# Loads that cast, transposes in column halves and masks on VectorE for the first three batches of an attention and mixer kernel

## The chip, the cores and the metric

The kernel runs on one core of a Trainium2 chip: TensorE (PE) for matrix products, VectorE (DVE), ScalarE (ACT) and GpSimd (POOL) for the rest, SyncE (SP) as a queue of DMAs, 16 DMA engines between HBM and the on-chip memory SBUF. Products land in PSUM, which is used here in eight banks. The metric is the time of one execution in microseconds of the device; less is better.

## The reference

Dilated sliding-window attention on 8 batches of 8 heads (576 positions, 64 per head), and an MLP mixer on its output. Heads 0 to 3 see the last 32 positions, heads 4 to 7 every fourth of the last 128. All inputs are fp32.

```python
B, H, S, D = q.shape                       # 8, 8, 576, 64
scores = (1 / np.sqrt(D)) * np.matmul(q, k.transpose(0, 1, 3, 2))
rel = pos[:, None] - pos[None, :]
mask_plain = (rel >= 0) & (rel < 32)                           # heads 0 to 3
mask_dil = (rel >= 0) & (rel < 128) & (rel % 4 == 0)           # heads 4 to 7
attn = softmax(where(mask, scores, -1e9)); x = attn @ v        # (B, S, 512) after joining heads
h = np.maximum(x.T @ w_tok1, 0) @ w_tok2                       # mixing over positions, 576 -> 256 -> 576
u = x + h.T
out = u + np.maximum(u @ w_ch1, 0) @ w_ch2                     # 512 -> 1536 -> 512
```

## The kernel before

Everything is computed in fp16 with fp32 sums. Positions 0 to 511 of a batch are kept in two orders: natural blocks of 128 for the first four heads and for columns 0 to 255, and four residues modulo 4 for the rest; the last 64 positions (the tails) are handled apart, for odd batches together with the batch before.

**A batch.** The loads bring q, k and v as fp32 tiles (`l_q`, `l_k`, `lt` for the tails, `l_vn`, `l_vd`, `l_vx`, `l_vt`), each line of q and k four positions or 1 KB long, v in part in lines of 256 bytes. Casts make fp16 tiles (`c_q`, `c_k`, `c_t`, `vv`, `vt`); copies and casts of all engines go through `copy` (L99 to 103). Then q and k are turned, so that the head's 64 numbers lie on partitions: by TensorE against an identity for batches 0 to 2, by DMA transposes from batch 3 on (`dma_steps`, `place_steps`). Scores are products of k and q blocks inside the band, ACT takes their exponentials into `attp` (plain heads), `attd` (dilated) and `attt` (tails); `values` multiplies by v and divides by the sum (`rec`, `xn`); `emit_h1`, `emit_u` and `emit_uT` do the mixing over positions and turn its result; `gen_first` (gp, gt) and `gen_second` (yp) are the two feed-forward products, the bulk of TensorE's work.

**Two forms of scores.** Batches 0 and 1 use `transposes`, `scores_plain` and `scores_dil`: q is laid out padded in `qz`, the other head's half being zero, so that one product has all 128 partitions, and the mask is a product that is put in ahead of each score (`veil`: the identity times a table of large negative numbers, L430). From batch 2 on, `scores_twin` gives the two heads of a pair to the two row halves of TensorE, unpadded (64 partitions each, L519), and GpSimd multiplies the exponentials by tables of 0 and 1 (`mult`, L113). Batch 2 is turned by `unpad`, four transposes of 128 x 128 for a pair of heads.

**Order.** The order of instructions on each engine is the order in which the program emits them. The opening (batch 0 up to its uT) is written out by hand (L843 to L973). Batch 0 loads through SP and ACT and is cast by ACT, VectorE and GpSimd. After that `interleave` (L819) runs a generator of feed-forward products as the main line and puts steps in between; each step has a due time, and each piece of the main line and each step moves the planner's clock by a cost. The stages are: gp of batch 0 with the attention and mixing of batch 1 (L1000 to L1005); gp of batch 1, yp of batch 0 and yp of batch 1 with batch 2, and with loads, casts, transposes and scores of batch 3 (L1007 to L1024); from there on one batch's gp and yp with the values and mixing of the next and the scores of the one after (L1026 to L1040). PSUM banks go round: `fl` and `main` have three, `sc` two. The weights come through GpSimd's queue, whose DMAs cast from fp32 to fp16 on the way (`load_w3`, `load_w4`, w1p, w2); a one-element copy (`gate`, L858) holds batch 1's loads behind w2. `w2p` is a reordered copy of w2.

Of the kernel before, what the change touches and what calls it, by code (L numbers as in the profile page):

```python
# [15 lines left out]
H = 8  # L16
# [53 lines left out]
def kernel(  # L70
# [14 lines left out]
    SRC = {"q": q, "k": k, "v": v}  # L85

# [24 lines left out]
    def mult(eng, out, a, b):  # L111
# [38 lines left out]
    w2p = [fixed(f"w2p_{i}", [128, 4, 128]) for i in range(2)]  # L150
# [47 lines left out]
    def load_v_steps(b):  # L198
        tn = sb.tile([128, 4, 4, D], FP32, tag="l_vn", bufs=1, name=f"l_vn_{b}")
# [15 lines left out]
        return steps  # L215

# [31 lines left out]
    c16 = {}  # L248

# [13 lines left out]
    def cast_vn(b, s, eng):  # L263
        copy(eng, vv[b % 2][:, s, 0:4, 0:64], l32[(b, "vn")][:, s])
# [3 lines left out]
    def cast_vd(b, h, eng):  # L268
        copy(eng, vv[b % 2][:, 0:4, 4 + h:6 + h, 0:64],
# [34 lines left out]
    def transposes(b, nm, hp):  # L304
        c = c16[(b, nm)]
        p = bank("fl" if b or nm == "q" else "main", 3, f"tp_{nm}_{b}_{hp}", FP16)
        grid = p[:, 0:4 * RS].rearrange("p (r i) -> p r i", i=RS)
        flat = nm == "k" or hp >= 2 or b == 0
        for r in range(4):
            nc.tensor.transpose(  # L310
                out=p[:, 128 * r:128 * r + 128] if flat else grid[:, r, 0:128],
                in_=c[:, hp, r].rearrange("m h d -> m (h d)"), identity=ident)
        main = p[:, 0:512].rearrange("p (r m) -> p m r", r=4)
        if nm == "k":
            nc.vector.tensor_copy(out=natural(kt[hp][:, 0:512]), in_=main)
# [755 lines left out]
```

## Time and profile before

| | us |
|---|---|
| median of 2 runs (285.93 to 286.45) | 286.19 |
| the profiled execution | 286.81 |
| its span on the core | 285.0 |
| PE busy | 273.8 |
| GpSimd busy | 166.8 |
| VectorE busy | 132.3 |
| ScalarE busy | 131.4 |

The span is what the trace covers, and the execution is 1.8 us longer. A row of a stretch gives its length, then for each engine busy time with the number of instructions, the granted clock of TensorE as a share of full speed, the mean busy share of 16 DMA engines (it can pass 1, since packets overlap) and what they moved. A row of instructions in time gives start, duration, engine, line, operation, what it writes and reads, shape and count; rows on PE name the part of the array in use (128*128; 64*128 are row halves, 128*64 column halves). A row of a group gives busy time and mean duration in ns, and then the idle time ahead of it with what ended it.

### The profile page before, as it was taken

To read this page: it belongs to the slowest core of one execution; us is meant where nothing else is said; L and a number is where in the kernel's file an instruction comes from. 1 tells how busy PE (TensorE), PEld (TensorE's weight loads), DVE (VectorE), ACT (ScalarE), POOL (GpSimd) and SP (SyncE) were. 2 spreads that over 40 slices of the span, in tenths; PEclk is the share of its full clock that TensorE was granted. 3 is DMA by queue.
4 is the path that set the end of the run, shared out by engine and by line. 5 is a ranking of instruction groups with operands and counts; after the bars stand their busy time and mean duration, and the time that the engine had idled before them with its cause. 6 is when DMAs were issued, how large, how long until landed. Compare 5 with 4: busy or idle time off the path is not lost.

```text
span 285.0 us, 6873 instructions
## 1 busy us (share of the span) xinstructions
PE 273.8 (96%) x2760; PEld 207.0 (73%) x2760; DVE 132.3 (46%) x280; ACT 131.4 (46%) x263; POOL 166.8 (59%) x236
## 2 busy tenths in 40 slices
PE   5799899999999999999999999999999999999994
PEld 2696576676896976598776976797767966886594
DVE  6875687652365155514730263526531184322022
ACT  2964563458412374473446625482456435134500
POOL 7980853383998769769945998289945900000000
PEclk9999999999999999999999999999999999999999
DMA  7999999999658999999798989399994310521032
GB/s 217 262 227 253 269 230 241 273 223 307 165 105 191 147 332 274 190 168 352 201 191 191 319 241 188 60 235 314 207 148 83 110 39 0 111 93 37 2 86 99
DMA packets 105423, 52.60 MB, mean 185 GB/s; under 512 B 73872, under 2 KB 104208, under 8 KB 105392
## 3 DMA queue, kind: packets, MB, share of 16 engines
q1 hardware_dynamic: 101280, 47.07, 71.2%
q0 software_dynamic: 2512, 3.92, 7.6%
q10 hardware_dynamic: 1600, 1.18, 1.4%
q8 instruction: 21, 0.34, 0.5%
q14 instruction: 10, 0.08, 0.1%
HBM read 37.05 MB, written 9.44 MB: 163 GB/s over the span
## 4 chain that ended last, share of the span: by engine, by line
PE 79%; DMA 9%; POOL 4%; ACT 2%; DVE 2%; issue 1%; SPq 1%; ACTq 0%; POOLq 0%
PE gp L767 26%; PE yp L790 26%; PE h1p L626 4%; PE up L638 4%; PE gt L758 4%; PE yp L810 4%; DMA l_k<-in_k_dram 3%; DMA lt<-in_k_dram 3%; PE sc L519 2%; DMA utm<-u 2%; DMA w<-in_moe_w_tok_dram 2%; POOL attd L113 1%; PE av L605 1%; PE h1p L624 1%; PE av L600 1%
## 5 line engine op out<-in xcount | busy, mean ns | idle before, releaser
L790 PE MATMUL yp<-w,gt 128*128 128x256 f16 x756 | 86.5, 273 | 0.0
L790 PEld LDWEIGHTS <-gt 128*128 128x128 f16 x768 | 78.4, 106 | 6.2
L107 ACT ACTIVATE gt<-gp 128x512 f16<-128x512 f32 x76 | 45.4, 601 | 68.6 <-PE gp L767 68.3
L767 PE MATMUL gp<-utm,w 128*128 128x512 f16 x192 | 67.7, 379 | 0.0
L767 PE MATMUL gp<-utd,w 128*128 128x512 f16 x144 | 54.8, 380 | 0.0
L767 PEld LDWEIGHTS <-w 128*128 128x128 f16 x384 | 39.0, 114 | 20.4 <-issue 1.9
L800 DVE TENSOR_TENSOR o<-yp,u 128x512 f32<-128x512 f32 x31 | 21.4, 691 | 66.5 <-PE yp L790 64.6
L113 POOL TENSOR_TENSOR attp<-attp,const 128x1280 f16<-128x1280 f16 x12 | 31.4, 2615 | 22.4 <-ACT attp L545 18.0
L113 DVE TENSOR_TENSOR xn<-av,rec 128x320 f16<-128x320 f32 x64 | 31.5, 492 | 2.2
L113 POOL TENSOR_TENSOR attd<-attd,const 128x1024 f16<-128x1024 f16 x12 | 25.3, 2129 | 2.4 <-ACT attd L545 2.4
L644 DVE TENSOR_TENSOR u<-up,xn 128x512 f16<-128x512 f32 x26 | 17.5, 689 | 14.1 <-PE up L638 14.0
L103 POOL CAST c_k<-l_k 128x512 f16<-128x512 f32 x29 | 18.0, 623 | 8.8 <-PE tpu L675 7.6
L107 ACT ACTIVATE h<-h1p 128x256 f16<-128x256 f32 x29 | 11.1, 383 | 26.0 <-PE h1p L626 25.7
L103 POOL CAST c_q<-l_q 128x512 f16<-128x512 f32 x31 | 19.6, 635 | 2.6 <-DMA l_q<-in_q_dram 2.6
L545 ACT ACTIVATE attp<-sc 128x480 f16<-128x480 f32 (+1 forms) x36 | 16.1, 528 | 7.4 <-PE sc L519 7.4
L109 DVE TENSOR_SCALAR gt<-gp 128x512 f16<-128x512 f32 x20 | 13.7, 686 | 10.1 <-PE gp L767 10.1
L103 POOL CAST vv<-l_vn 128x256 f16<-128x256 f32 (+1 forms) x40 | 15.0, 403 | 4.0 <-DMA l_vn<-in_v_dram 3.5
L373 POOL COPY kt<-kr 128x512 f16<-128x512 f16 x10 | 10.8, 1079 | 10.4 <-DMA kr<-c_k 6.6
L697 ACT COPY utd<-utm 128x512 f16<-128x512 f16 x12 | 12.7, 1123 | 9.0 <-DMA utm<-u 9.0
L615 DVE RECIPROCAL rec<-av 128x5 f32<-128x5 f32 x64 | 12.2, 190 | 7.4 <-PE av L612 7.0
L545 ACT ACTIVATE attd<-sc 128x512 f16<-128x512 f32 x24 | 12.4, 604 | 6.1 <-PE sc L519 6.1
L758 PEld LDWEIGHTS <-w 128*128 128x128 f16 x192 | 11.9, 113 | 2.0 <-issue 0.4
(149 smaller groups left out, 441.2 us busy)
## 6 DMA issues: line engine op xcount, KB each, us to landing
out_dram<-o SPq DMA_DIRECT2D x72, 128.0 KB, 2.7
l_q<-in_q_dram SPq DMA_DIRECT2D x15, 512.0 KB, 6.9
l_k<-in_k_dram SPq DMA_DIRECT2D x14, 512.0 KB, 7.4
l_vn<-in_v_dram SPq DMA_DIRECT2D x32, 128.0 KB, 6.7
l_vd<-in_v_dram SPq DMA_DIRECT2D x16, 256.0 KB, 4.3
w<-in_moe_w_ch_dram POOLq DMA_DIRECT2D x6, 512.0 KB, 8.3
lt<-in_q_dram SPq DMA_DIRECT2D x8, 128.0 KB, 5.0
l_vt<-in_v_dram SPq DMA_DIRECT2D x8, 128.0 KB, 4.6
```

Source lines behind the costliest of these rows:

```text
L103: eng.tensor_copy(out=out, in_=in_)
L107: nc.scalar.activation(out=out, in_=in_, func=AF.Relu)
L109: eng.tensor_scalar_max(out=out, in0=in_, scalar1=0.0)
L113: eng.tensor_tensor(out=out, in0=x, in1=y, op=ALU.mult)
L545: nc.scalar.activation(out=out, in_=in_, func=AF.Exp, scale=0.125)
L615: nc.vector.reciprocal(out=rec[:, :, 0], in_=av[:, :, 64])
L644: nc.vector.tensor_tensor(out=u16(b, s), in0=blocks4(p), in1=blocks4(xn[b][:, s]), op=ALU.add)
L697: nc.scalar.copy(out=natural(uTd[:, cb - 2]), in_=uTm[i][:, cb].rearrange("p r m -> p m r"))
L758: nc.tensor.matmul(out=p[:, 128 * i:128 * i + 128], lhsT=w3_block(cb, 4 * g + i), rhs=uT[(b, cb)][1], start=(cb == order[0]), stop=(cb == ...
L767: nc.tensor.matmul(out=p, lhsT=w3_block(cb, mb), rhs=uT[(b, cb)][0], start=(i == 0), stop=(i == 3))
L790: nc.tensor.matmul(out=p[:, c], lhsT=gta[:, mb, a0:m0 + 512:4] if half else gta[:, mb, a0:a0 + 128], rhs=w4[mb][:, c], start=(mb == 0), st ...
L800: nc.vector.tensor_tensor(out=blocks4(o32), in0=blocks4(p), in1=u16(b, s), op=ALU.add)
```

## The change

- Batch 0: heads 0 to 3 of q and k, the tails, the natural blocks of v and the residues of v are still loaded as fp32 by SP and ACT and cast by engines; heads 4 to 7 of q and k, the rest of v come by GpSimd's DMAs, which cast. Batches 1 and 2: all q and k, tails and v come by GpSimd's casting DMAs (`early_loads`), but the residues of v, which are loaded there as fp32 and cast by ACT or GpSimd. The tiles of the three batches take the place of other batches' fp32 tiles.
- `unpad` turns batches 0 to 2 with 64 transposes of [128, 64] each batch, a head of the pair in each column half.
- `transposes`, `scores_plain`, `scores_dil`, `qz`, `veil` and their products are gone. Batches 0 and 1 use the unpadded scores (class `Scores`, with steps of its own for batch 0), and VectorE multiplies by the masks; batch 2 keeps GpSimd for it.
- `w2p` is gone; the products read w2 with a stride of 4. Some relus and sums go to another engine; batch 1 has one summed product where it had two (the identity times xn, then copied by ACT).
- The opening is a list of steps sorted by place; its memsets are spread over VectorE and GpSimd; GpSimd makes the identity instead of loading it.
- The products go by batch: gp and yp of batch 0 with the attention and mixing of batch 1, then gp and yp of batch 1 with batch 2 and the scores of batch 3. All weights are issued in the opening's list. From batch 2's products on nothing changes.

The function `order`, of which the code is full, only records and asserts the order of emission; it emits nothing.

```diff
+    def early_qk(b, nm, h0, h1):
+        nc.gpsimd.dma_start(
+            out=c16[(b, nm)][:, h0:h1].rearrange("m h r d -> m h (r d)"),
+            in_=SRC[nm][b, h0:h1, 0:512, :].rearrange("h (m r) d -> m h (r d)", r=4))
+    def early_vn(b, s):
+        nc.gpsimd.dma_start(out=vv[b % 2][:, s, 0:4, 0:64],
+                            in_=v[b, 0:4, 128 * s:128 * s + 128, :].rearrange("h s d -> s h d"))
+    def early_loads(b):
+        return [lambda: (new_early(b), early_tail(b, "q")), lambda: early_tail(b, "k"),
+                lambda: early_qk(b, "q", 0, 4), lambda: early_qk(b, "k", 0, 4),
+                lambda: early_qk(b, "q", 4, 8), lambda: early_qk(b, "k", 4, 8),
+                lambda: early_vn(b, 0), lambda: early_vn(b, 1), lambda: early_vn(b, 2), lambda: early_vn(b, 3),
+                lambda: early_vt(b), lambda: early_vd(b, 0), lambda: early_vd(b, 2), lambda: early_vx(b)]
...
     def unpad(b, nm, hp, eng):
-        p = bank("fl", 3, f"tp_{nm}_{b}_{hp}", FP16)
+        p = bank("main" if b == 0 and nm == "k" else "fl", 3, f"tp_{nm}_{b}_{hp}", FP16)
         for r in range(4):
-            nc.tensor.transpose(out=p[:, 128 * r:128 * r + 128],
-                                in_=c[:, hp, r].rearrange("m h d -> m (h d)"), identity=ident)
+            for h in range(2):
+                nc.tensor.transpose(out=p[64 * h:64 * h + 64, 128 * r:128 * r + 128], in_=c[:, 2 * hp + h, r],
+                                    identity=ident)
...
+        def mask(self, j):
+            hp, eng = 2 * self.g + j, self.masks[j]
+            if self.g == 0:
+                w = plain_blocks(hp)[:, :, :, 0:BLK]
+                mult(eng, w, w, band)
+    def scores_twin(b, g):
+        s = Scores(b, g, None, (nc.vector,) * 3 if b == 1 else None)
...
-                        out=p[:, c], lhsT=w2p[jb][:, s] if half else w2[jb][:, 128 * s:128 * s + 128],
+                        out=p[:, c], lhsT=w2[jb][:, s:512:4] if half else w2[jb][:, 128 * s:128 * s + 128],
...
+    S0 = [Scores(0, 0, (("sc", 2), ("sc", 2), ("main", 3), ("main", 3), ("fl", 3), ("fl", 3)), (DVE, DVE, DVE)),
+          Scores(0, 1, (("sc", 2), ("sc", 2), ("sc", 2), ("sc", 2), ("fl", 3), ("fl", 3)), (DVE, DVE, DVE))]
+    opening = [
+        (0, lambda: early_qk(0, "q", 4, 8)),
+        (0, lambda: early_qk(0, "k", 4, 8)),
+        (5.0, make_ident),
+        (0, seen),
...
+        (23.0, lambda: load_w3(0)),
+        (20.0, lambda: load_w3(1)),
+        (24.0, lambda: load_w3(2)),
+        (25.0, e1[2]),
...
+        (29.0, lambda: load_w4(0)),
+        (23.0, lambda: load_w4(1)),
+        (30.0, lambda: load_w4(2)),
...
+        (25.0, lambda: S0[0].mask(1)),
+        (30.0, va[0]),
...
+    interleave(None, [(p, 0.0, f) for p, f in opening])
...
-    interleave(gen_first(0), steps)
+    steps = turn_steps(1, (6.8, 8.0, 6.4, 8.4, 11.6, 11.7, 8.8, 12.2, 5.0, 9.0),
+                       (nc.scalar, nc.scalar, nc.vector, nc.vector, nc.scalar, nc.scalar, nc.scalar, nc.vector))
+    steps += score_steps(1, 9.5, 4.1)
+    va = value_steps(1, 19.8, 0.6)
+    steps += mix_steps(1, 26.0, 28.5, 30.5, 36.0, 0)
+    steps += at(16.0, 2.0, e2)
+    def first_both():
+        yield from gen_first(0)
+        yield from gen_second(0)
+    interleave(first_both(), steps)
+    def second_both():
         yield from gen_first(1)
-        yield from gen_second(0)
         yield from gen_second(1)
...
+    steps += score_steps(2, 6.0, 4.0)
+    steps += value_steps(2, 13.5, 1.0)
+    steps += mix_steps(2, 16.5, 21.0, 22.0, 37.0)
+    steps += at(8.0, 0.0, [lambda: emit_loads_qk(3)]) + at(9.0, 0.0, [lambda: load_v(3)])
+    steps += at(11.6, 0, cast_steps(3)) + at(12.6, 0.6, dma_steps(3)) + at(19.8, 0.5, place_steps(3))
+    steps += score_steps(3, 28.0, 4.0) + at(22.0, 1.5, load_steps(4))
+    interleave(second_both(), steps)
```

More of the change, by code (lines that the diff above doesn't have):

```diff
@@ L85 @@
     SRC = {"q": q, "k": k, "v": v}
+    SP, ACT, DVE, POOL = nc.sync, nc.scalar, nc.vector, nc.gpsimd
     def fixed(name, shape, dtype=FP16):
@@ L198, in load_v_steps @@
     def load_v_steps(b):
+        order((b, "load v"), *([(b - 2, "vd", h) for h in (0, 2)] + [(b - 2, "values", h) for h in range(8)]))
         tn = sb.tile([128, 4, 4, D], FP32, tag="l_vn", bufs=1, name=f"l_vn_{b}")
@@ L263, in cast_vn @@
     def cast_vn(b, s, eng):
+        order((b, "vn", s), *([("load vn", s)] if not b else []))
         copy(eng, vv[b % 2][:, s, 0:4, 0:64], l32[(b, "vn")][:, s])
@@ L268, in cast_vd @@
     def cast_vd(b, h, eng):
+        order((b, "vd", h), *([(b, "load vd", h)] if b < 3 else []), *([(b - 2, "values", 4 + h + i) for i in range(2)] if b > 1 else []))
         copy(eng, vv[b % 2][:, 0:4, 4 + h:6 + h, 0:64],
@@ L396, in turn_tails @@
     def turn_tails(b, eng):
+        order((b, "t"), "ident", *([(b - 1, "small", hp) for hp in range(4)] if b else ["cast t"]))
         p = bank("fl", 3, f"tp_t_{b}", FP16)
@@ L590, in values @@
         hp, i = h // 2, h % 2
+        order((b, "values", h), (b, "mask", hp), (b, "mask tails", hp // 2), ("ones", b % 2))
+        if b < 3:
+            order(None, (b, "vt"), *([("zeros", i) for i in range(2)] + [(b, "vn", s) for s in range(4)] if hp < 2 else [(b, "vx"), (b, "vd", 2 * (hp - 2))]))
+            if hp < 2 and b:
+                order(None, (b, "twice"))
         odd = b % 2
@@ L618, in emit_h1 @@
     def emit_h1(b, jb, half, t):
+        order((b, "h1", jb, half), ("w1", half), ("w1t", b % 2), *[(b, "values", h) for h in range(4 * half, 4 * half + 4)])
         x = xn[b]
@@ L950, in u_half @@
         for jb in range(2):
-            lhsT = w2p[jb][:, s] if half else w2[jb][:, 128 * s:128 * s + 128]
-            nc.tensor.matmul(out=p, lhsT=lhsT, rhs=h1[jb][:, c], start=(jb == 0 and not summed),
+            lhsT = w2[jb][:, s:512:4] if half else w2[jb][:, 128 * s:128 * s + 128]
+            nc.tensor.matmul(out=p, lhsT=lhsT, rhs=h1s[0][jb][:, c], start=(jb == 0 and not summed),
                              stop=(jb == 1))
         if summed:
-            nc.scalar.copy(out=t, in_=blocks4(p))
+            copy(ACT, t, blocks4(p))
@@ new lines, in cast_first_tails, with seen, w1t_zeros @@
+    def cast_first_tails(eng):
+        order("cast t")
+        copy(eng, c16[(0, "t")], lt0)
+    def seen():
+        order("seen")
+        POOL.memset(attt, 1.0)
+    def w1t_zeros(i, eng):
+        order(("w1t zeros", i))
+        eng.memset(w1t[i], 0.0)
+    first_load("q", 0, SP)
+    first_load("k", 0, ACT)
+    first_load("q", 2, SP)
+    first_load("k", 2, ACT)
+    lt0 = sb.tile([128, H, D], FP32, tag="lt", bufs=1, name="lt_0")
+    l32[(0, "t")] = lt0
+    load_tail(0, "q", SP)
+    load_tail(0, "k", ACT)
```

628 lines of the change are left out of this document (287 added, 341 removed).

## The prediction

> **What bounds the kernel now.** I read the page first, then the stretches between stages, then TensorE's instructions in order of time.
>
> ```profile
> span 285.0 us, 6873 instructions
> PE 273.8 (96%) x2760; PEld 207.0 (73%) x2760; DVE 132.3 (46%) x280; ACT 131.4 (46%) x263; POOL 166.8 (59%) x236
> ...
> core 0: us, PE busy (x) PEld busy (x) DVE busy (x) ACT busy (x) POOL busy (x), PEclk, DMA share, GB/s
> ...
> 6.70:26.10 19.40, 17.48 (x252) 14.90 (x252) 14.74 (x38) 12.98 (x30) 12.92 (x31) 1.00 1.19 238
> 26.10:54.60 28.50, 26.72 (x296) 18.45 (x293) 20.59 (x45) 14.51 (x30) 13.79 (x26) 1.00 1.12 254
> 54.60:103.30 48.70, 48.18 (x521) 38.58 (x519) 19.89 (x42) 22.14 (x48) 36.88 (x49) 1.00 0.88 204
> 103.30:285.00 181.70, 177.86 (x1694) 133.86 (x1691) 72.50 (x150) 79.73 (x155) 98.46 (x123) 1.00 0.70 162
> ```
>
> TensorE is busy 96% of the span at full clock (1.00), but its ends are modelled, so I count its work by steps from start to start. The stretches are cut where the feed-forward products of batch 0, 1 and 2 begin:
>
> ```profile
> 26.11 3.48 PE L767 MATMUL gp<-utm,w 128*128 128x512 f16 x14
> ...
> 54.62 3.71 PE L767 MATMUL gp<-uT,w 128*128 128x512 f16 x16
> ...
> 72.08 3.44 PE L790 MATMUL yp<-w,gt 128*128 128x256 f16 x30
> ...
> 103.26 0.38 PE L767 MATMUL gp<-utd,w 128*128 128x512 f16 x1
> ...
> PE tp_q L310 <- POOL c_q L103: 0.7, 2, 0.5
> ```
>
> So there are three parts. The **opening** runs to 26.1. The **middle**, 26.1 to 103.3, is 77.2 us. The **rest**, 181.7 us, isn't touched by the change. In the rest nothing is left for it to win, so the forecast is the opening and the middle.
>
> Steps of TensorE, from the starts below: 512 columns 0.216 (114.81 to 115.03), four transposes 0.22 (8.87 to 9.09), a veil with its product 0.14, 0.11 and 0.06 at 160, 128 and 64 columns.
>
> ```profile
> 8.87 0.39 PE L310 MATMUL tp_q<-const,c_q 128*128 128x128 f16 x4
> 9.09 0.39 PE L310 MATMUL tp_k<-const,c_k 128*128 128x128 f16 x4
> ...
> 32.88 0.23 PE L430 MATMUL sc<-veil,const 128*128 128x160 f16 x1
> ...
> 33.02 0.23 PE L430 MATMUL sc<-veil,const 128*128 128x160 f16 x1
> ...
> 37.11 0.19 PE L430 MATMUL sm<-veil,const 128*128 128x64 f16 x1
> ...
> 37.17 0.19 PE L430 MATMUL sm<-veil,const 128*128 128x64 f16 x1
> ...
> 38.60 0.22 PE L430 MATMUL sc<-veil,const 128*128 128x128 f16 x1
> ...
> 38.71 0.22 PE L430 MATMUL sc<-veil,const 128*128 128x128 f16 x1
> ```
>
> By columns (0.216 us for 512, the small ones as above) the middle holds: products of batches 0 and 1, 46.9; batch 1's attention and mixing, 14.4; batch 2's, 9.2; batch 3's scores, 1.6. That is 72.0 of 77.2, so **5.2 us are stalls**. Batch 1's part has 3.7 of them (10.4 for gp of batch 0 and 14.4 fill 24.8 of its 28.5 us), behind loads and casts: the DMA share is 1.12 there, and the wait of a transpose for GpSimd's cast is the longest one named.
>
> **The change part by part.**
>
> *Scores of batches 0 and 1.* Before, a batch has 12 veiled pairs of 160 columns, 20 of 128 and 12 of 64: 12 x 0.14 + 20 x 0.11 + 12 x 0.06 = 4.6 us. After, it has the form that batch 3 has here, two heads in two row halves:
>
> ```profile
> 91.28 0.65 PE L519 MATMUL sc<-qt,kt 64*128 64x160 f16 x14
> ...
> 91.98 6.72 PE L790 MATMUL yp<-w,gt 128*128 128x256 f16 x60
> 98.63 0.62 PE L519 MATMUL sc<-qt,kr 64*128 64x128 f16 x16
> ...
> 99.30 4.12 PE L790 MATMUL yp<-w,gt 128*128 128x256 f16 x36
> ```
>
> That is 0.70 + 0.67, with 0.1 on entering each, 1.6 us. It saves 3.0 us a batch on TensorE, and with one summed product less (4 to 2 of 256 columns, 0.2) the middle loses 3.2 us of work.
>
> *Transposes of batches 0 to 2 in two column halves.* They go from 32 to 64 a batch, each half as wide in stationary columns. The only column halves in this trace are those of the tail products:
>
> ```profile
> 114.81 0.38 PE L767 MATMUL gp<-utd,w 128*128 128x512 f16 x1
> 115.03 0.38 PE L767 MATMUL gp<-utm,w 128*128 128x512 f16 x1
> 115.34 0.62 PE L648 MATMUL up<-h,w 128*64 128x512 f16 x4
> 115.89 0.41 PE L767 MATMUL gp<-utd,w 128*128 128x512 f16 x1
> ```
>
> Four of them take 0.55 to the next start, not 4 x 0.216 = 0.86: two run side by side. Against 2 x 0.216 that leaves 0.12, and the first starts 0.09 late (0.31 after the gp before it), so a visit to that form costs 0.21 more. I take the transposes at their old 0.22 for four, plus 0.21 a visit. By the places given, batch 1's eight groups fall into about four visits between products and batch 2's into about three: 7 x 0.21 = 1.5 us more in the middle. The ends are 0 (all beside row halves) and 16 visits plus no overlap, 16 x (0.21 + 0.22) = 6.9.
>
> *Masks.* GpSimd's row is the one mask row of before, and VectorE's rate must come from its copies:
>
> ```profile
> L113 POOL TENSOR_TENSOR attp<-attp,const 128x1280 f16<-128x1280 f16 x12 | 31.4, 2615 | 22.4 <-ACT attp L545 18.0
> ...
> L315 DVE COPY kt<-tp_k 128x512 f16<-128x512 f16 x4 | 2.7, 689 | 0.9 <-PE tp_k L310 0.9
> ...
> L103 DVE COPY utm<-tpu 128x512 f16<-128x512 f16 x2 | 0.8, 424 | 0.1
> ...
> 53.88 0.49 DVE L103 COPY uT<-tpu 128x640 f16<-128x640 f16 x1
> ...
> 15.53 0.20 DVE L615 RECIPROCAL rec<-av 128x5 f32<-128x5 f32 x1 [0.30 <-PE av L612]
> ...
> 16.17 0.18 DVE L615 RECIPROCAL rec<-av 128x5 f32<-128x5 f32 x1
> ...
> 23.69 1.08 DVE L957 TENSOR_TENSOR u<-up,xn 128x256 f16<-128x256 f32 x3
> ```
>
> 128 elements more cost a copy 0.07, so 1280 elements are 0.42 + 6 x 0.07 = 0.84 and 1024 are 0.70; the upper end is the slow copy's pace, 0.69 x 2.5 = 1.7. I take the lower, since mask and scores lie in order in SBUF. A batch's masks are then 2 x 0.84 + 2 x 0.70 + about 0.65 for the tails = 3.7 us of VectorE.
>
> *The opening.* VectorE was busy 14.7 of 19.4 us there. After, from about 7 us (the identity is made by GpSimd behind a memset, three DMA issues and a cast, so transposes start about where they did, 6.7), it has: a cast, 0.35; zeros, about 1.1; two k copies at 0.69; q and dilated k, 4 x 0.42 + 2 x 0.28; tails, ends and their cast, 1.3; masks 3.7; two casts of v, 0.5; eight heads of values at 0.64 (15.53 to 16.17), 5.1; two relus 0.8; four sums at 0.36, 1.4; two uT copies 0.8. That is 18.7 us without a gap, and the stretch after the last values has some 2 us of VectorE waits for TensorE now and keeps them. 6.6 + 18.7 + 1.9 = 27.2: the opening ends **1.1 later**, although TensorE has 3 us less to do. **VectorE becomes its bound.** Ends: 25.0 (its waits gone, quicker strided copies) and 30 (slow masks).
>
> *Order and loads of the middle.* Batch 1's attention gets the products of both gp and yp of batch 0 beside it (20.8 us instead of 10.4), and batch 2's gets 26 instead of 36. The first should shorten the 5.2 us of stalls, the second bring some back, with the masks of batch 2 and the casts of batch 3 (11 and 10 us of GpSimd) now squeezed into 38 us. At the end of each part h1, relu, u and uT still run without cover. I take 1 us more stall in all, between -4 and +4.
>
> The fp32 casts of batches 1 and 2 leave GpSimd (17 a batch, up to 0.63 each, about 10 us), and 14 DMA issues at up to 0.76 come in their place, also about 10; w2p's copies go. That is off the path, as long as data arrive. The second weights w4 are needed at about 27 + 16 = 43 us, not at 72:
>
> ```profile
> q1 hardware_dynamic: 14048, 7.22, 69.4%
> q0 software_dynamic: 2110, 2.47, 32.0%
> q10 hardware_dynamic: 1600, 1.18, 8.9%
> ...
> 15.35 0.76 POOL L863 DMA_DIRECT2D w<-in_moe_w_ch_dram  x1
> ...
> L103 POOL CAST c_q<-l_q 128x512 f16<-128x512 f32 x31 | 19.6, 635 | 2.6 <-DMA l_q<-in_q_dram 2.6
> ```
>
> The shares are of the first 45 us. GpSimd's casting queue wrote 2.47 MB, so read 4.94, in 14.4 us: 343 GB/s. The plain queue did 231. Ahead of the last w4 in the new order stand about 13.8 MB of reads, some 10.2 on the casting queue: 29.7 + 3.6/0.231 = 45.3 us of DMA time, and as the shares add up to 1.11, they land near 41 + 2 = 43. It is just in time, so I cost it at nothing, with no slack left.
>
> **Sum** against the profiled execution (286.81, 1.8 of it around the span; the median 286.19 lies 0.6 below): +1.1 opening, -3.2 scores and sum, +1.5 visits, +1.0 stalls = **+0.4**, so 287.2, and 286.6 by the median. I say **287**.
>
> **The rivals.**
>
> 1. *Late data, slower.* The casting queue's rows get short: v rows of 256 bytes are written as 128. If the extra 6 MB of reads go at the plain queue's 231 GB/s instead, the sum is 23 + 25.5 us over 1.11, w4 lands at 46 and batch 1's v at 50; if short rows halve that once more, some 4 to 8 us are lost in stage two and again ahead of batch 2. From 5.3 us of lateness on it is over 2%. For it: DMA share above 1 up to 70 us. Against: weights needed less DMA time a byte on this very queue. Price +4 to +8: 291 to 295. [...]
>
> 2. *The stalls go, faster.* Batch 1's inputs come with no cast behind them, and 20.8 us of products cover their turn. Stalls fall from 5.2 to 1.5, the opening ends at 26: -0.1 - 3.2 + 1.5 - 3.7 = -5.5, and at fewer visits -6.5: 280 to 281. For it: waits on casts are those named in batch 1's part. Against: the chain of h1, u and uT at the end of each part is as uncovered as before.
>
> 3. *The halves don't overlap.* A transpose is four times shorter than the tail product, and its weight load might not hide. 16 x 0.22 = +3.5 in the middle, some of it in the opening: 290 to 291. [...]
>
> **How the numbers follow.** Forecast 0.52, late data 0.2, stalls gone 0.18, no overlap 0.1. About 2% (5.7 us) is what a measurement can tell here: faster is below 280.5, slower above 291.9. Most of rival 2 lies about that lower line and gives 0.15; rival 1 gives 0.18 above, with little from slow masks: 0.2. The forecast's own range is 283 to 291. With the stalls' ends and the nearer parts of the rivals the range is 280 to 294.
>
> **What would show it.** Right: VectorE at nine tenths from 7 to 26 us and gp of batch 0 starting at 26 to 28; twin scores of 1.6 us in batches 0 and 1; each group of eight transposes in 0.22, about 0.43 with its visit; gp of batch 2 starting 102 to 105. Wrong: a wait of yp for w4 or of values for a v load (rival 1); transposes 0.1 apart in pairs (rival 3); gp of batch 2 before 99 (rival 2). If gp of batch 0 starts before 24, VectorE wasn't the opening's bound.

## The result, and the profile after

The changed kernel takes 293.68 us (median of 2 runs, 293.58 to 293.78) against 286.19: a ratio of 1.0262, 95% interval 1.0218 to 1.0306. It is slower by 7.5 us. The forecast was 287; the measured time lies inside the range (280 to 294), near its upper end. The page of its profiled execution:

```profile
span 292.1 us, 6853 instructions
...
PE 273.3 (94%) x2766; PEld 203.7 (70%) x2766; DVE 129.2 (44%) x285; ACT 134.2 (46%) x271; POOL 165.9 (57%) x218
...
PEclk9559999999999999999999999999999999999999
```

TensorE is as busy as before (273.3 against 273.8 us), though the veils and their work are gone. (It has 2766 instructions against 2760, since the transposes are twice as many and half as wide.) The last row says part of why: in the second and third of 40 slices, 7.3 to 21.9 us, it was granted half its clock. Before it had 1.00 there. The same four parts as before, cut at the first gp of batch 0, 1 and 2:

```profile
core 0: us, PE busy (x) PEld busy (x) DVE busy (x) ACT busy (x) POOL busy (x), PEclk, DMA share, GB/s
6.96:29.76 22.80, 18.15 (x240) 14.13 (x240) 17.19 (x46) 11.60 (x28) 14.05 (x25) 0.70 1.34 210
29.76:66.21 36.45, 34.78 (x378) 25.09 (x376) 20.54 (x44) 18.04 (x39) 16.26 (x23) 1.00 1.25 197
66.21:110.43 44.22, 39.16 (x456) 28.96 (x453) 17.44 (x39) 21.99 (x50) 32.95 (x38) 1.00 0.64 147
110.43:292.10 181.67, 177.88 (x1692) 134.39 (x1691) 71.79 (x149) 79.81 (x153) 96.83 (x122) 1.00 0.66 159
```

The opening ends at 29.76 instead of 26.11, **3.65 later**. The middle takes 36.45 + 44.22 = 80.67 instead of 77.15, **3.5 more**. The rest, 181.67, is unchanged. In the middle TensorE is busy for 73.94 us (34.78 + 39.16) and was for 74.85 (26.73 + 48.12, cut at its own starts of gp); its idle time went from 2.30 to 6.73. So the middle didn't get more work, it got holes.

*The opening.* The clock of the changed kernel in stretches, and two of the same stretches of the kernel before:

```profile
7.00:8.00 1.00, 1.00 (x32) 1.00 (x31) 0.83 (x3) 0.00 (x0) 0.91 (x2) 0.82 1.22 188
...
8.00:10.00 2.00, 0.87 (x12) 0.31 (x7) 1.51 (x3) 0.99 (x2) 1.55 (x4) 0.50 1.34 221
10.00:12.00 2.00, 0.67 (x8) 0.48 (x10) 0.45 (x2) 0.62 (x2) 0.89 (x3) 0.50 1.43 255
...
18.00:20.00 2.00, 2.00 (x28) 1.62 (x27) 1.56 (x5) 1.56 (x4) 0.61 (x1) 0.50 1.19 207
20.00:22.00 2.00, 1.91 (x26) 1.51 (x25) 1.79 (x6) 0.89 (x3) 0.74 (x1) 0.68 1.69 183
22.00:24.00 2.00, 1.59 (x23) 1.34 (x22) 1.90 (x7) 0.69 (x2) 1.88 (x3) 1.00 1.28 217
```

```profile
8.00:10.00 2.00, 1.73 (x24) 1.49 (x24) 1.46 (x4) 1.59 (x4) 1.68 (x6) 1.00 1.10 333
10.00:12.00 2.00, 1.84 (x28) 1.55 (x27) 1.88 (x6) 1.89 (x4) 2.00 (x5) 1.00 1.31 250
```

The first busy figure of a row is TensorE's, the third from the end its clock. From 8 to 12 us it was busy for 1.54 of 4 us, before for 3.57. TensorE's instructions in order of time show the gap ahead of that, and the price:

```profile
1.26 3.35 PE L800 MATMUL idle_p<-idle 128*128 128x512 f16 x8 [1.26 <-DVE idle L900]
6.96 0.41 PE L407 MATMUL tp_q<-ident,c_q 128*64 128x128 f16 x8 [2.35 <-POOL ident L168]
...
19.31 1.90 PE L844 MATMUL w_p<-w1p,spread 128*128 128x256 f16 x8
...
22.59 1.03 PE L844 MATMUL w_p<-w1p,spread 128*128 128x256 f16 x8
```

The warm-up (eight products of an idle tile, first row) ends at 4.6, then TensorE waits 2.35 us for GpSimd's identity. The same eight products w_p take 1.90 us at half clock and 1.03 at the full one.

*The middle.* Waits of TensorE from 66 to 111 us (us in total, times, longest):

```profile
PE gp L729 <- ACT utd L668: 1.6, 1, 1.6
PE h1p L593 <- DVE xn L114: 0.8, 1, 0.8
PE gp L729 <- ACT attt L447: 0.7, 1, 0.7
PE tp_k L407 <- ACT attp L447: 0.6, 1, 0.6
PE sc L465 <- POOL kt L392: 0.6, 1, 0.6
PE av L577 <- POOL attt L114: 0.5, 1, 0.5
```

What stands behind the first, fifth and sixth is seen in GpSimd's and SP's queues:

```profile
75.81 2.62 POOL L114 TENSOR_TENSOR attp<-attp,const 128x1280 f16<-128x1280 f16 x1 [20.91 <-DVE kt L104]
...
87.49 1.14 POOL L114 TENSOR_TENSOR attt<-attt,const 128x512 f16<-128x512 f16 x1
88.59 0.60 POOL L104 CAST c_t<-lt 128x512 f16<-128x512 f32 x1
```

```profile
101.34 5.97 SPq L658 DMA_TRANSPOSE utm<-u  x1
```

GpSimd stood idle for 20.9 us, then had batch 2's masks from 75.8 to 88.6 and only behind them batch 3's casts. SP's transpose of batch 2's u was issued at 101.34, took 5.97 us to issue (1.6 in later stages) and landed at 109.3; before it was issued at 94.03.

### The profile page after: what moved, and what is told of

The parts are those of the page before. It is cut to its first block, busy times and chain, and to the rows that moved or that the text cites. A ratio compares the mean times of both kernels' runs of the same rounds, so it can differ in the third digit from the quotient of the medians.

```text
span 292.1 us, 6853 instructions
## 1 busy us (share of the span) xinstructions
PE 273.3 (94%) x2766; PEld 203.7 (70%) x2766; DVE 129.2 (44%) x285; ACT 134.2 (46%) x271; POOL 165.9 (57%) x218
## 4 chain that ended last, share of the span: by engine, by line
PE 78%; DMA 7%; POOL 5%; ACT 3%; SPq 2%; DVE 2%; issue 1%; ACTq 0%; POOLq 0%
PE gp L729 26%; PE yp L752 25%; PE h1p L595 4%; PE up L608 3%; DMA lt<-in_k_dram 3%; PE gt L720 3%; PE sc L465 3%; PE yp L772 3%; DMA utm<-u 3%; ACT attp L447 1%; DMA l_vn<-in_v_dram 1%; POOL attd L114 1%; PE av L568 1%; PE av L573 1%; PE h1p L593 1%
## 5 line engine op out<-in xcount | busy, mean ns | idle before, releaser
L108 ACT ACTIVATE gt<-gp 128x512 f16<-128x512 f32 x79 | 47.3, 604 | 70.0 <-PE gp L729 69.7
L729 PE MATMUL gp<-utm,w 128*128 128x512 f16 x192 | 66.5, 379 | 0.5 <-ACT gt L108 0.5
L729 PEld LDWEIGHTS <-w 128*128 128x128 f16 x384 | 39.4, 114 | 25.5 <-issue 5.2
L114 POOL TENSOR_TENSOR attp<-attp,const 128x1280 f16<-128x1280 f16 x12 | 31.4, 2614 | 40.3 <-DVE kt L104 20.9
L447 ACT ACTIVATE attp<-sc 128x480 f16<-128x480 f32 (+1 forms) x48 | 21.6, 524 | 11.3 <-PE sc L465 11.2
L614 DVE TENSOR_TENSOR u<-up,xn 128x512 f16<-128x512 f32 x27 | 18.1, 689 | 11.4 <-PE up L608 11.1
L447 ACT ACTIVATE attd<-sc 128x512 f16<-128x512 f32 x32 | 16.7, 606 | 7.6 <-PE sc L465 7.6
L608 PE MATMUL up<-h,w 128*128 128x256 f16 x112 | 16.5, 273 | 0.0
L110 DVE TENSOR_SCALAR gt<-gp 128x512 f16<-128x512 f32 x17 | 11.7, 687 | 9.8 <-PE gp L729 9.8
L668 ACT COPY utd<-utm 128x512 f16<-128x512 f16 x12 | 12.6, 1120 | 6.3 <-DMA utm<-u 6.3
L104 POOL CAST c_k<-l_k 128x512 f16<-128x512 f32 x21 | 12.9, 616 | 0.0
L729 PE MATMUL gp<-uT,w 128*128 128x512 f16 x48 | 12.3, 381 | 0.7 <-ACT attt L447 0.7
```

Source lines behind the costliest of these rows:

```text
L104: eng.tensor_copy(out=out, in_=in_)
L108: nc.scalar.activation(out=out, in_=in_, func=AF.Relu)
L110: eng.tensor_scalar_max(out=out, in0=in_, scalar1=0.0)
L114: eng.tensor_tensor(out=out, in0=x, in1=y, op=ALU.mult)
L447: nc.scalar.activation(out=out, in_=in_, func=AF.Exp, scale=0.125)
L608: nc.tensor.matmul(out=p[:, c], lhsT=w2[jb][:, s:512:4] if half else w2[jb][:, 128 * s:128 * s + 128], rhs=h1[jb][:, c], start=(jb == 0 an ...
```

## The experiments

All cuts in one table: start of gp of batch 0, length of the two middle stages (gp of batch 0 to gp of batch 1, and from there to gp of batch 2), the rest, and the median; us. The ratio is to runs of the kernel before taken in the same round.

| kernel | gp 0 | stage 2 | stage 3 | rest | median | ratio to before |
|---|---|---|---|---|---|---|
| before | 26.11 | 28.51 | 48.64 | 181.7 | 286.19 | 1 |
| changed | 29.76 | 36.45 | 44.22 | 181.7 | 293.68 | 1.0262 (1.0218 to 1.0306) |
| e1 idle products | 27.82 | 36.45 | 43.48 | 181.7 | 291.47 | 1.0211 (1.0170 to 1.0253) |
| e2 identity early | 29.20 | 36.44 | 44.02 | 181.6 | 293.64 | 1.0283 (1.0233 to 1.0334) |
| e3 u turned first | 29.20 | 36.44 | 42.42 | 181.7 | 292.11 | 1.0208 (1.0189 to 1.0227) |
| e5 masks of batch 2 | 29.03 | 36.45 | 41.27 | 182.1 | 290.31 | 1.0146 (1.0118 to 1.0174) |
| e7 combined, loads reordered | 34.96 | 36.45 | 40.91 | 182.5 | 295.29 | 1.0323 (1.0296 to 1.0350) |
| e9 the same, identity early | 34.15 | 36.44 | 40.91 | 182.4 | 294.82 | 1.0287 (1.0257 to 1.0317) |
| e10 three mends | 28.21 | 36.45 | 40.91 | 182.4 | 289.35 | 1.0112 (1.0092 to 1.0131) |
| e12 three mends, late k | 27.84 | 36.45 | 40.90 | 182.4 | 289.36 | 1.0113 (1.0090 to 1.0135) |
| e11 three mends, pairs by DMA | 27.70 | 39.01 | 40.15 | 182.4 | 291.05 | 1.0174 (1.0150 to 1.0198) |
| e8 full-width transposes | 27.56 | 35.71 | 40.14 | 182.4 | 287.56, one run | |
| e4 before, early warm-up | 26.48 | 28.09 | 48.64 | 181.5 | 286.71 | 1.0023 (1.0005 to 1.0041) |
| e13 before, no veils | 26.21 | 27.34 | 48.67 | 182.5 | 286.87 | 1.0016 (1.0002 to 1.0030) |

**Idle products in the opening.** The theories were: the clock costs the opening its time, or late data and VectorE do.

```
-        (0, lambda: warm(8)),
+        (0, lambda: warm(18)),
+        (13.0, lambda: fill(S0[0], 0, 2)),
         (13.0, lambda: S0[0].main(0)),
...
+        (13.0, lambda: fill(S0[0], 2, 6)),
         (13.0, lambda: turn_tails(0, DVE)),
...
+        (29.0, lambda: fill(S0[1], 4, 8, 256)),
         (29.0, lambda: S0[1].small(1)),
```

> The changed kernel with 26 more idle products in the gaps of the opening: 18 instead of 8 at the start (until about 6.8 us, where the first transposes begin), two ahead of the first scores, six ahead of the tails' transposes, eight narrow ones ahead of the last small scores. Clock theory: TensorE's granted clock stays at 1.00 from 7 to 22 us, where the changed kernel had 0.50 from 7.8 to 21.3; the eight spread-weight products take 0.9 instead of 1.7 us, the values' products 0.03 a step instead of 0.055; gp of batch 0 starts at 27.5 to 28.8 instead of 29.76, and the run takes 291 to 292.5 us against 293.7. Data theory (the opening waits for casts, the tails' load and VectorE's masks): the clock stays up as well, but h1p and gp of batch 0 move by less than 0.4 us, 293.3 to 294. If the clock falls all the same, the fillers were too thin and the run says nothing on its price.

The clock stayed at 1.00, and gp of batch 0 came at 27.82, 1.94 earlier. (Three runs took 291.10 to 291.75 us, one 293.53.) Two stretches of this kernel:

```profile
6.96:12.00 5.04, 4.24 (x57) 2.09 (x56) 2.83 (x7) 1.62 (x3) 3.17 (x9) 1.00 1.36 234
12.00:23.00 11.00, 9.03 (x159) 7.17 (x156) 10.68 (x32) 7.83 (x19) 8.50 (x15) 1.00 1.35 205
```

The clock theory holds for 1.9 of the 3.65 us. What is left, 1.7, goes with the data theory: until 12 us VectorE (third busy figure) has 2.83 us of work in 5.04, and 1.2 of its idle 2.2 us are the wait for the tails' load, which lands at about 11; from 12 to 23 it is busy for 10.68 of 11.00. With the clock up, VectorE is the bound.

**Identity early.**

```
-        (5.0, make_ident),
-        (0, seen),
-        (0, load_const),
+        (0, make_ident),
+        (0, seen),
+        (0.5, load_const),
...
-        POOL.memset(attt, 1.0)
+        DVE.memset(attt, 1.0)
```

> The changed kernel with the identity made first on GpSimd, ahead of the attt fill, which goes to VectorE (idle there from 2.7 to 6 us), and GpSimd's cast of the first k ahead of the load of the constants. Data theory: the identity is there at about 3.6 us instead of 6.9, the first transposes start at about 5 instead of 6.96, the first scores at 6.5 to 7.2 instead of 8.98; the tails' cast still waits for its load (10.8 us), so the opening gains 0.3 to 1.2 us: gp of batch 0 at 28.6 to 29.5, the run 292.5 to 293.4. Clock theory: the gap of 2.35 us ahead of the first transposes goes, but TensorE is as sparse between 7 and 12 us as before, so the clock still falls to 0.50, only later (10 to 12 us), and the run stays within 0.5 of 293.7.

gp of batch 0 came at 29.20, inside the data theory's 28.6 to 29.5, but the run took 293.64 (293.16 to 296.42) and the clock fell all the same, from about 8.6 to 15.4 and again from 18.8 to 22.2: the tails' load still left TensorE idle (1.8 us of waiting for their cast). An early identity alone buys nothing that can be told from the scatter of the clock. That scatter is itself a finding. The next kernel, e3, has the changed kernel's opening; three of TensorE's rows, then three stretches:

```profile
10.70 0.61 PE L422 MATMUL tp_t<-ident,c_t 128*128 128x128 f16 x4 [0.91 <-DVE c_t L104]
...
13.18 0.64 PE L407 MATMUL tp_q<-ident,c_q 128*64 128x128 f16 x8
...
14.17 0.41 PE L407 MATMUL tp_k<-ident,c_k 128*64 128x128 f16 x8
```

```profile
16.00:18.00 2.00, 1.17 (x23) 0.88 (x24) 1.97 (x7) 0.72 (x4) 2.00 (x4) 0.85 1.22 207
18.00:20.00 2.00, 2.00 (x22) 1.64 (x22) 1.60 (x6) 1.57 (x3) 0.32 (x1) 0.50 1.20 211
20.00:22.00 2.00, 1.53 (x30) 1.30 (x28) 1.76 (x6) 1.11 (x2) 0.86 (x2) 0.80 1.69 180
```

If the clock is either 0.50 or 1.00 (the changed kernel's trace records no other value), the means 0.85 and 0.80 put it at half from 17.4 to 20.8, 3.4 us. Every row of e3 ahead of that reads 1.00, but the products don't bear this out. The four transposes tp_t take 0.61 us, as in the changed kernel at 0.50, and 0.40 in e1; eight half-width transposes take 0.64 at 13.18 and 0.41 at 14.17. The clock rose between these two, and a row shows 1.00 ahead of a trace's first record of the clock, as it does in the changed kernel, whose first record is at 4.23 us. So here the eight warm-up products had not raised the clock, and behind 6.96 us it was at half for 6.2 to 7.2 us and then for 3.4, about 10 us in all. In the changed kernel it was half from 7.6 to 21.3, 13.7 us; in e2, and by its rows in e5, 6.8 + 3.4 = 10.2. The start of gp of batch 0 follows: 29.76 after 13.7 us of half clock, 29.03 to 29.20 after about 10, and 27.56 to 28.21 in the five kernels (e1, e8, e10, e11, e12) that have the idle products and no half clock there.

**The transpose of u ahead of the loads** (stage 3).

```
-            for t, tail in ((2.0, True), (6.0, False))[1 - b % 2:]:
+            for t, tail in ((2.0, True), (6.0 if b > 2 else 4.0, False))[1 - b % 2:]:
...
-    steps += score_steps(3, 28.0, 4.0) + at(22.0, 1.5, load_steps(4))
+    steps += score_steps(3, 28.0, 4.0) + at(26.5, 1.2, load_steps(4))
```

> The changed kernel with the DMA transpose of batch 2's u put into SP's queue ahead of all of batch 4's loads instead of behind its first five (the loads from 26.5 in steps of 1.2 instead of from 22 in steps of 1.5). Queue theory: the transpose is issued at 97.5 to 98.5 us instead of 101.34, its issue takes 1.6 to 3 us instead of 5.97 and it lands before 104 instead of 109.3; the 1.63 and 0.17 us for which gp of batch 2 waited go, gp starts at 108.5 to 109, the run takes 291.7 to 292.3 us. Rival (the transpose is slow because of the stores and casts that share the DMA engines, not because of the loads ahead of it): it lands at 105 to 108, which still hides behind the second products, or the loads of batch 4 come late and the gain is lost in the next stage: 293 to 294.

```profile
97.40 1.72 SPq L658 DMA_TRANSPOSE utm<-u  x1
```

The issue took 1.72 instead of 5.97 us, and gp of batch 2 waited for nothing: stage 3 is 1.80 shorter, as the queue theory forecast. Stores and casts share the DMA engines as before; what moved are the loads ahead of it in SP's queue, four of them by the trace of the changed kernel (both tails, a q and a k), not five. In the kernel before, with two loads ahead, the issue took 3.46. Whether the loads hold the transpose up in the queue or on the DMA engines that both use, no run tells apart.

**Masks of batch 2 on VectorE.**

```
-        s = Scores(b, g, None, (nc.vector,) * 3 if b == 1 else None)
+        s = Scores(b, g, None, (nc.vector,) * 3 if b in (1, 2) else None)
```

> The changed kernel with batch 2's five masks on VectorE, as in batches 0 and 1, instead of on GpSimd. Mask theory: GpSimd's chain from 75.8 to 88.6 us (2.6, 0.7, 2.6, 4.2 and 1.1 us of masks) is what batch 2's values and batch 3's casts wait for; on VectorE the masks take 0.88, 0.28, 0.88, 1.4 and 0.42 and are done by about 82, the waits of h1p for xn (0.81) and of the values for attt (0.50) go, and so does that of batch 3's scores for kt (0.58), since the casts start 6 us earlier; the span falls by 1.2 to 2.2 us, to 291.5 to 292.5. Queue theory: the same waits go, but the transpose of batch 2's u still lands at 109 and gp of batch 2 waits longer for it, 3 us instead of 1.63; the run stays at 293 to 293.8.

```profile
106.75 0.38 PE L729 MATMUL gp<-utd,w 128*128 128x512 f16 x1 [0.20 <-ACT utd L668]
```

Stage 3 is 2.95 shorter, more than the mask theory's 1.2 to 2.2. The waits for GpSimd's kt and for batch 2's attt are gone; h1p still waits 0.8 for xn, against that theory. The queue theory's longer wait for utd didn't come: the transpose is issued at 98.75, 2.6 us earlier, and gp waits 0.2 twice. The mends of e3 and e5 overlap: 1.80 and 2.95 apart, 3.31 together (below).

**All three, and the loads reordered.** Beside the edits of e1, e3 and e5:

```
-    first_load("q", 2, SP)
-    first_load("k", 2, ACT)
     lt0 = ...
     load_tail(0, "q", SP)
     load_tail(0, "k", ACT)
+    first_load("q", 2, SP)
+    first_load("k", 2, ACT)
```

> The changed kernel with the idle products of the first experiment, the transpose of u ahead of the loads, batch 2's masks on VectorE, and the loads of batch 0's last q and k rows ahead of those of its second two heads. If the three causes add up: gp of batch 0 at 27.82 us or, where the tails' load was what the opening still waited for, at 26.8 to 27.4; 36.45 us from there to gp of batch 1, 40.7 to 41 to gp of batch 2 (44.22 in the changed kernel, 41.27 with the masks moved and 42.42 with the transpose moved: most of the two gains is the same wait); 181.7 behind it; a span of 285.8 to 287 and 287.4 to 288.7 us a run, still 1 to 2.5 above before. Rival: VectorE, with three more masks and the last rows early, becomes what the values wait for: 289.5 or more.

The middle came out as added up (36.45 + 40.91), the opening failed: gp of batch 0 at 34.96. The two displaced loads, which the next casts wait for, on VectorE and on ScalarE:

```profile
10.37 0.43 DVE L104 CAST c_k<-l_k 128x512 f16<-128x512 f32 x1 [7.71 <-DMA l_k<-in_k_dram]
```

```profile
12.87 0.62 ACT L102 CAST c_q<-l_q 128x512 f16<-128x512 f32 x1 [7.43 <-DMA l_q<-in_q_dram]
```

In the changed kernel these casts start at 6.02 and 5.62. Placing 128 KB a queue ahead of the loads made them 4.4 and 7.3 us later. That GpSimd's own loads, issued from 1.3 us on, got ahead of them is my reading; no run took it apart. The clock fell here too, in spite of the idle products: to 0.50 from 12.6 to 19.5 us, so not all of the 7 us lost in the opening need be the loads'. With the identity early as well:

> The combined kernel with the identity and the first cast of k early as well, as in the second experiment. There the identity did come early and the opening did not gain. If the tails' load was what held it, the two together give 0.5 to 1 us: gp of batch 0 at 26.2 to 27, 286.5 to 288 us a run. If VectorE's copies, masks and normalizations hold it from 12 us on, gp of batch 0 stays within 0.3 of the combined kernel's.

34.15: neither forecast holds. Both kernels have the reordered loads, and here too the clock was at 0.50 for 6.8 us (11.9 to 18.7).

**The three mends alone**: the idle products, the transpose of u ahead of the loads, and batch 2's masks on VectorE, with the changed kernel's load order.

> The combined kernel with batch 0's loads in the changed kernel's order again: the idle products, the transpose of u ahead of the loads, and batch 2's masks on VectorE alone. In the combined kernel the pieces behind the opening came out as expected (36.45 and 40.91 us), and the reordered loads cost 7 us in the opening. If the three causes are the changed kernel's loss: gp of batch 0 at 27.6 to 28, 36.45 and 40.9 us behind it, gp of batch 2 at 105 to 105.4 (before 103.26), a span of 286.6 to 287, 288 to 288.8 us a run, 1.006 to 1.010 of before. If they interact (the earlier opening brings loads and stores together), the middle is over 78 us and the run over 289.

gp of batch 2 at 105.57, 0.2 above the forecast, but 289.35 us, above 288 to 288.8. Of TensorE's waits behind 104 us one is new:

```profile
PE av L577 <- POOL attt L114: 0.9, 1, 0.9
```

Batch 3's masks are on GpSimd too, and with stage 3 shorter its values come up before they are done. Every kernel with batch 2's masks moved shows it (a rest of 182.1 to 182.5): 0.4 to 0.8 us of the mend is given back.

**Late k.** The load of the last heads of k behind the attt fill.

```
         (0, lambda: early_qk(0, "q", 4, 8)),
-        (0, lambda: early_qk(0, "k", 4, 8)),
         (5.0, make_ident),
         (0, seen),
+        (0, lambda: early_qk(0, "k", 4, 8)),
```

> The three mends, with the load of batch 0's last four heads of k issued by GpSimd behind its fill of attt, 2.3 us later. With the clock up, VectorE runs without a gap from 12 us (behind the tails' load, which lands at 10.8 to 11) to 23. Tails theory: the load shares its engines with 256 KB less, lands at 9.5 to 10.3, and all of VectorE's chain moves up by as much: gp of batch 0 at 26.9 to 27.5, 287.3 to 288 us a run. Rival: the late k lands at 12.5 to 13.5 instead of about 10.5, its transposes (13.8 in the run with idle products) and the scores behind them wait, or the fill, the identity and the first cast stand 0.7 earlier and nothing else moves: 288 to 289.

gp of batch 0 at 27.84 and 289.36 us: no gain. The tails' cast did start earlier, at 10.40 against 11.05 in e1, but the six idle products stood ahead of the tails' transposes, which started at 11.57. My own fillers hid the effect, so this run doesn't settle what the tails' load costs.

**Column form.** Full-width transposes of neighbouring columns, beside the three mends, to price the visits. They mix the positions up, so only the time of this kernel counts.

```
-            for h in range(2):
-                nc.tensor.transpose(out=p[64 * h:64 * h + 64, 128 * r:128 * r + 128], in_=c[:, 2 * hp + h, r],
-                                    identity=ident)
+            nc.tensor.transpose(out=p[:, 128 * r:128 * r + 128], in_=flat[:, 512 * hp + 128 * r:512 * hp + 128 * r + 128], identity=ident)
```

> As the combined kernel without the reordered loads, with each pair's eight half-width transposes of batches 0 to 2 replaced by four of full width on neighbouring columns (they read the same bytes and mix the positions up, so the products are of other numbers). It prices the column form. By the prediction 0.21 us a visit and seven to eight visits in each of the batches 1 and 2: 1.5 us less between gp of batch 0 and gp of batch 2. By the changed kernel's own rows (eight halves in 0.32 to 0.35 us against four whole ones in 0.22 to 0.24): 0.1 a visit, 1.5 to 1.7 over the 16 visits of both batches in all, 0.8 in each of the two stages. Rival: the visits lie beside other waits, and it gives less than 0.4.

0.74 and 0.77 us less than in e10: 1.51 together, as the prediction had it. TensorE in the same place, column halves (e10), then full width:

```profile
35.87 1.05 PE L729 MATMUL gp<-utm,w 128*128 128x512 f16 x4
36.85 0.41 PE L407 MATMUL tp_k<-ident,c_k 128*64 128x128 f16 x8
37.20 0.62 PE L729 MATMUL gp<-utm,w 128*128 128x512 f16 x2
37.76 0.41 PE L407 MATMUL tp_k<-ident,c_k 128*64 128x128 f16 x8
```

```profile
35.00 1.03 PE L727 MATMUL gp<-utm,w 128*128 128x512 f16 x4
35.86 0.39 PE L406 MATMUL tp_k<-ident,c_k 128*128 128x128 f16 x4
36.09 0.59 PE L727 MATMUL gp<-utm,w 128*128 128x512 f16 x2
36.52 0.39 PE L406 MATMUL tp_k<-ident,c_k 128*128 128x128 f16 x4
```

From start to start the transposes take 0.35 against 0.23, and the products ahead of a visit 0.98 against 0.86 (four) and 0.56 against 0.43 (two). A visit costs 0.12 in itself and 0.12 in what stands ahead of it, 0.24. By e10's trace the middle has eight visits (five in stage 2, three in stage 3), so 0.19 on average; some stand behind a wait.

To get full width with the right data, the cast loads of batches 1 and 2 were written in the order of pairs:

```
+        if b:
+            for h in range(h0, h1):
+                nc.gpsimd.dma_start(out=c16[(b, nm)][:, h // 2, :, h % 2],
+                                    in_=SRC[nm][b, h, 0:512, :].rearrange("(m r) d -> m r d", r=4))
+            return
```

> The three mends, with the cast loads of q and k of batches 1 and 2 written into the order of pairs (one load a head, 128 bytes a piece, instead of one for four heads with 512 bytes a piece), so that each visit takes four full-width transposes. The full-width kernel measured what the column form costs: 0.74 and 0.77 us in the two stages. If the loads' price hides in GpSimd's idle time, 35.7 and 40.1 us: gp of batch 2 at 103.4 to 104, 286.5 to 287.3 us a run. Rival (16 issues of 0.75 us a batch instead of 4, and short pieces): GpSimd is 9 us longer at the loads of batch 1, whose values and the weights w4 behind them come late in a stage that has 1.7 us of idle; 289 to 294.

Stage 3 gained (40.15), stage 2 took 39.01, by one wait ahead of all others:

```profile
PE yp L761 <- DMA w<-in_moe_w_ch_dram: 3.0, 2, 1.9
```

That is the prediction's first rival, late w4, brought about by another load order: the issues ahead of w4 are 16 instead of 4, and their pieces 128 bytes instead of 512. Which of the two pushes w4 back wasn't told apart. In the changed kernel there is no such wait.

**On the kernel before.** An earlier warm-up (the fill of the idle tile on VectorE, first), and the veils left out, so that the scores of batches 0 and 1 are unmasked:

```
-        nc.gpsimd.memset(idle, 0.0)
+        nc.vector.memset(idle, 0.0)
```

> The kernel before with the fill of the idle tile on VectorE ahead of all else, so that its eight warm-up products run from about 1.3 to 4.7 us, as in the changed kernel, and TensorE stands still for 2 us until the first transposes at 6.7. If that gap alone lowers the clock: 0.50 for 7 to 14 us from about 8 on, gp of batch 0 1 to 3 us later than 26.11, 287 to 289 us a run. If it takes the sparse work behind the gap too (before keeps TensorE busy for 0.80, 1.73 and 1.84 of each 2 us from 6 to 12, the changed kernel for 1.04, 0.87 and 0.67), the clock stays at 1.00 and the run within 0.5 of before.

```
-        if hide is not None:
-            nc.tensor.matmul(out=out, lhsT=ident, rhs=hide, start=True, stop=False)
...
-                         start=hide is None, stop=True)
+                         start=True, stop=True)
```

> The kernel before without its 88 veil products: the scores of batches 0 and 1 are left unmasked, and nothing masks them in their place. By steps of TensorE that is 2.3 us a batch, half of the 4.6 that a batch's scores take. If that work was on the path, gp of batch 0 starts at 24 to 25 instead of 26.11, gp of batch 1 2 us sooner after it (28.5 to 26.5), and the run takes 282 to 284 us. Clock theory: the veils were what kept TensorE busy between 7 and 12 us; with half the work there the clock falls to 0.50 for one or more stretches of 3.4 us between 8 and 20, as in the changed kernel, and the opening gains nothing: gp of batch 0 at 25.5 to 27, 284 to 286. Cover theory: the 2.3 us of batch 1 lie beside casts and loads, the stalls grow by what the work shrinks, and the middle stays within 1 us of 77.15.

With the gap alone the clock falls, but for one stretch:

```profile
8.00:10.00 2.00, 1.88 (x16) 1.89 (x17) 0.81 (x3) 1.19 (x3) 1.89 (x7) 0.56 1.10 326
10.00:12.00 2.00, 1.77 (x18) 1.48 (x17) 1.35 (x4) 1.33 (x3) 2.00 (x5) 0.58 1.29 260
```

By the reckoning of e3's rows that is half clock from 8.2 to 11.7, 3.4 us, between two forecasts. My reading is that the gap (1.9 us ahead of the first transposes) brings the fall and the dense work behind it (3.65 of the 4 us from 8 to 12) ends it; no run took these apart. Of the ten executions six have a mean clock of 0.992 to 0.994, as this one has; those of the kernel before have 0.997 to 1.000. It cost 0.4 in the opening, which stage 2 took back. Without the veils the clock stayed at 1.00 in the profiled execution, and nine of ten executions have a mean of 0.997 or more (one has 0.992). So the veils' loss isn't by itself what lowers it; in the changed kernel the gap and the sparse stretch behind it go together. The starts of gp without veils:

```profile
26.21 3.48 PE L765 MATMUL gp<-utm,w 128*128 128x512 f16 x14
...
53.55 3.71 PE L765 MATMUL gp<-uT,w 128*128 128x512 f16 x16
...
102.22 0.38 PE L765 MATMUL gp<-utd,w 128*128 128x512 f16 x1
```

2.3 us of TensorE's work a batch taken out gave nothing in the opening, 1.17 in stage 2, and the rest grew by 0.7. The run is no shorter (1.0016). From 101 to 140 us TensorE has one wait that the kernel before hasn't, for GpSimd's copy ahead of the scores of batch 4:

```profile
PE sc L517 <- POOL kt L373: 0.7, 1, 0.7
```

That copy had itself waited 2.50 us for a DMA transpose of k. So work that came 1.0 us earlier met the next batch's data late, as in e10. The cover theory is the nearest: the middle is 76.0, 1.1 below 77.15 where it said 1.

## Why the prediction was wrong by 6.7 us

That the range held the result is in part luck. The opening's upper end, 30, was given for slow masks, and VectorE's masks weren't slow; the range's upper end was stretched for late loads, and no product waits for w4. Only the stalls had an end (+4) for the cause that came, and they pass it. Three signs named for being right failed: gp of batch 0 started at 29.76 (26 to 28 was named), gp of batch 2 at 110.43 (102 to 105), and VectorE was busy for 14.57 of the 19.00 us from 7 to 26 (nine tenths was named).

The likeliest case, 287, failed, by two terms:

- **Opening, +1.1, measured +3.65.** That VectorE becomes the bound was right: at full clock it has 10.68 of 11.00 us between 12 and 23, and the five kernels with the idle products and the changed kernel's first loads start gp of batch 0 at 27.56 to 28.21, so +1.5 to +2.1. The size was off because VectorE's 18.7 us were laid without a gap from 6.6 us on, while it waits for the tails' load until 10.84. The other 1.9 are the clock by e1, and the starts grow with the time at half clock (above); that is a step that the prediction doesn't have: it read 1.00 in every row of before and kept it, though the change takes work away where TensorE is least busy and starts the warm-up 1.3 us sooner.
- **Stalls of the middle, +1.0, measured +4.4** (idle 2.30 to 6.73). The working named it, "the masks of batch 2 and the casts of batch 3 now squeezed into 38 us", and gave it 1 us of a range of -4 to +4, which the result leaves. By the runs the masks on GpSimd and the transposed u behind the loads are 44.22 - 40.91 = 3.3 of it. The remaining 1 us or so is open. It isn't in stage 2, whose idle time is 1.67 us (36.45 - 34.78) against 1.78 before. With the three mends, stage 3 still waits 0.8 for xn, 0.7 and 0.6 for exponentials and 0.3 for a copy of k (e10), and no run took these apart.

The two terms are 2.55 and 3.4 of the 6.7. Most of what is left is the work of the middle: scores, sum and visits were forecast at -1.7, and TensorE's busy time there fell by 0.9.

The other steps:

- *Scores, -3.0 a batch.* The twin scores of batch 1 take 0.70 + 0.67 between starts, as forecast; but the sum put all of the saving on the path, and the kernel without veils shows that about half stays in stage 2 and the end of the run is no earlier, since TensorE then waits 0.7 for the next batch's k. Lost as cover, as the prediction feared for stalls in general but didn't price here.
- *Visits, +1.5.* 1.51 measured, over eight visits where seven were forecast; 0.24 in a visit between products against 0.21. The third rival (halves that don't overlap) is out: at full clock eight halves take 0.22 to the next start (6.96 to 7.18 in the changed kernel), the price that the prediction took for four whole ones.
- *Masks.* On VectorE 1280 elements took 0.92 and 1024 took 0.69 (means of four), forecast 0.84 and 0.70.
- *w4 just in time, at no cost.* Right: yp of batch 0 starts at 45.09 without a wait. One more load order (e11) and it costs 3.0. The first rival's working has a slip: of its 23 + 25.5 us, the 23 are 7.9 MB at 343 GB/s, and these hold the 3.6 MB of the plain queue. With those at 231 GB/s the sum is 12.5 + 41.1 us, and w4 lands near 50 instead of 46; the rival didn't come at either. That short rows halve the queue's rate once more, on which its price rests, no run shows by itself; with pieces of 128 bytes instead of 512 for q and k of batches 1 and 2, the queue's packets took 28.4% of 16 engines' span instead of 22.4% for the same 8.7 MB (e11 against e10), 82.2 us instead of 64.5.
- *The rest unchanged.* Right, 181.7; but it isn't independent of the middle: it gives back up to 0.8 when gp of batch 2 comes early.
- The second rival (stalls go) is out: they doubled and more.

Of the sum, -0.7 was forecast for the middle and +3.5 came; +1.1 for the opening and +3.65 came.

## What to carry to other kernels

Take a saving on the path only as far as something else isn't late next: the veils' 2.3 us a batch on an engine that is busy 96% of the span gave 0 at the end of the run (e13). When work moves forward, follow the in-order queues, GpSimd's masks and the transposes behind loads on SP, with their own start times, since a part that is compressed by a quarter finds them where the sum has none. And when a change thins TensorE's work early in a kernel, price the clock: here a gap of 2.35 us and a sparse stretch behind it cost 1.9 us by e1.

## What the hardware showed that I hadn't expected

The granted clock fell to 0.50 in the opening and stayed there for 13.7 us in the changed kernel, 6.8 and 3.4 in e2 and e5, 3.4 in e3 and in e4. It didn't fall in e1, where idle products filled the gaps, but it did, for 6.8 us, in e7 and e9, which have the same idle products and later loads. With one order of the opening, that of the changed kernel, e3 and e5, it differed from execution to execution; in e3 the eight warm-up products, 3.6 us long, didn't even raise it. A row's 1.00 says nothing ahead of a trace's first record of the clock (4.23 us in the changed kernel, whose eight warm-up products took 0.42 each in rows of 1.00, where products of that shape take 0.22 at full clock); there the duration of like products tells it. From a fall to the next rise the stretches at 0.50 were 3.4, 6.8 and 13.7 us long, about one, two and four times 3.4; in the 3.4 us ahead of the changed kernel's fall (4.23 to 7.64) TensorE was busy for 1.06 us. What sets these lengths, and why the same order differs from execution to execution, no run shows.

A DMA transpose on SP took 5.97 us to issue behind four loads, 3.46 behind two (before) and 1.6 to 1.7 without them; and a load placed ahead of others on a hardware queue came with casts of those that started 4.4 and 7.3 us later (e7), where the 256 KB of the two queues would take 1.2 us at the 223 GB/s that e7 moved from 2 to 6 us.
